# Batch 0's q as f32 at the head of SyncE's queue, ahead of two constants, in a kernel that streams weights through GpSimd's queue

## Chip, cores, metric

One core of a Trainium2 chip. The sets of rounds ran on different chips, each with its own runs of the kernel before; the traces compared below are therefore not all of one chip. The metric is device time in microseconds (us) of one execution. A profile's span is the time from its first to its last instruction, about 1.8 us less than that run's device time. KB and KB/us count 1024 bytes; the profile's GB/s count 10^9.

## The reference, cut to what matters

```python
def _attn_ref(q, k, v):                       # 8 batches, 8 heads, 576 rows, 64 wide
    phi = lambda x: np.where(x > 0, x, np.exp(x) - 1.0) + 1.0
    q_p, k_p = phi(q), phi(k)
    kv = np.einsum('bhsd,bhse->bhde', k_p, v)
    z = np.sum(k_p, axis=2)
    num = np.einsum('bhsd,bhde->bhse', q_p, kv)
    den = np.einsum('bhsd,bhd->bhs', q_p, z)[..., None] + 1e-06
    return num / den
# then, on x = the attention's rows (8, 576, 512): rfft along the rows, the first 64 modes
# each multiplied by its own complex 512 x 512 matrix (w_r, w_i), irfft, and u + relu(u @ w_ch)
```

The 128 matrices of the modes are f32 in HBM: 134 MB of the 164 MB that the profile counts as read.

## The kernel before

GpSimd's queue loads everything large, and converts from f32 to 16 bits while it loads: 24 loads for q, k and v of 8 batches, then 128 matrices. The head of the kernel:

```python
    nc.vector.memset(actwarm, 0.0)
    nc.scalar.activation(out=actwarm, in_=actwarm, func=AF.Exp)
    nc.sync.dma_start(out=id16, in_=id16_dr.ap())           # 32 KB
    nc.sync.dma_start(out=fwd_sb, in_=fwd_dr.ap())          # 160 KB
    # ... cut ...
    def load(b):
        for nm, src in (("q", q), ("k", k), ("v", v)):
            t = sA.tile([128, NHP, NJ * Dh], F16, tag=f"{nm}16", bufs=2, name=f"{nm}16_{b}")
            pin(nc.gpsimd.dma_start(out=t, in_=src[b].rearrange(...)))
            raw[nm, b] = t
    # ... cut: exps(b): ScalarE, phi = exp(raw); features(b): VectorE, raw = max(raw, 0) + 1,
    #          then phi = min(phi, raw); turn_q, sum_kv, form_x, transform: TensorE ...
    load(0)
    load(1)
    exps(0)
    for _ in features(0):
        pass
    exps(1)
    for b in range(B):
        if b + 2 < B:
            load(b + 2)
            if b >= 1:
                w_next()          # a weight matrix behind each batch's loads
        # ... cut ...
```

The modes follow: 8 + 12 buffers for the matrices, each load waiting for a buffer that TensorE has done with. In the last three modes matmuls without use fill TensorE's waits:

```python
    def keep_warm(n: int):
        for _ in range(n):
            pin(nc.tensor.matmul(last_ps[0], id16, wch16[:, 0, :]))

    FILL = {61: (2, 2, 1), 62: (5, 3, 3), 63: (6,)}
```

The last mode's product (`y_last`) is followed by the inverse transform, the relu and the stores.

## Time and profile before

| | before |
|---|---|
| time, median of 3 runs | 428.85 us (428.75 to 429.17) |
| span of the profiled run | 427.4 us |
| first byte on SyncE's queue, on GpSimd's | 1.71, 2.91 us |
| last weight byte on GpSimd's queue | 393.98 us |
| from the end of the last mode's product to the end | 32.8 us |

From the page of the kernel before, the DMA rows of its 40 slices (busy tenths, and GB/s moved), and the shares of the chain that ended last:

```profile
DMA  8999999999999999999999999999999999996698
GB/s 146 207 208 209 209 210 209 211 214 214 218 212 214 213 214 213 215 212 214 213 213 214 213 214 212 214 214 214 214 213 214 214 214 212 213 213 135 211 404 313
...
q0 software_dynamic: 32256, 82.26, 99.0%
q1 hardware_dynamic: 3568, 9.78, 6.0%
...
DMA 73%; PE 12%; DVE 6%; issue 5%; POOL 1%; ACT 1%; DVEq 0%; POOLq 0%
```

"software_dynamic" is GpSimd's queue and "hardware_dynamic" SyncE's. Only the first slice and three of the last four are not full: the first moves 146 GB/s where the later ones of the stream move 207 and more, and that is all the slack the stream has. The chain is DMA for 73%.

The timeline of the kernel before, 0 to 12 us (start, duration, engine, line, operation; in brackets the idle time before it and what ended it):

```profile
0.74 0.34 SPq L85 DMA_DIRECT2D id<-ident  x1
1.14 0.42 SPq L86 DMA_DIRECT2D fwd_sb<-dft_fwd  x1
1.26 0.90 POOL L164 DMA_DIRECT2D q<-in_q_dram  x1 [0.82 <-POOLq L820]
2.15 0.77 POOL L164 DMA_DIRECT2D k<-in_k_dram  x1
...
8.15 2.22 ACT L182 ACTIVATE qe<-q 128x1152 f16<-128x1152 f16 x2 [5.92 <-DMA q<-in_q_dram]
10.40 0.76 DVE L189 TENSOR_SCALAR q<-q 128x2304 f16<-128x2304 f16 x1 [8.89 <-ACT qe L182]
11.05 2.22 ACT L182 ACTIVATE ke<-k 128x1152 f16<-128x1152 f16 x2 [0.68 <-DMA k<-in_k_dram]
11.20 1.43 DVE L195 TENSOR_TENSOR qe<-qe,q 128x1152 f16<-128x1152 f16 x2
```

Nothing is computed before 8.15 us: q, issued first, lands only then. That is what invites the change.

The chain of the kernel before, from 388 us:

```profile
378.90 15.36 DMA wi<-in_moe_w_i_dram
394.27 0.05 issue
394.31 0.30 PE y_last L391 x4
394.61 0.02 issue
394.64 0.23 DVE YT L402
```

The last load ends at 394.27 us, and the last four matmuls of the last mode wait for it.

### The profile page before, as it was taken

To read this page: it belongs to the slowest core of one execution; us is meant where nothing else is said; L and a number is where in the kernel's file an instruction comes from. 1 tells how busy PE (TensorE), PEld (TensorE's weight loads), DVE (VectorE), ACT (ScalarE), POOL (GpSimd) and SP (SyncE) were. 2 spreads that over 40 slices of the span, in tenths; PEclk is the share of its full clock that TensorE was granted. 3 is DMA by queue.
4 is the path that set the end of the run, shared out by engine and by line. 5 is a ranking of instruction groups with operands and counts; after the bars stand their busy time and mean duration, and the time that the engine had idled before them with its cause. 6 is when DMAs were issued, how large, how long until landed. Compare 5 with 4: busy or idle time off the path is not lost.

```text
span 427.4 us, 6617 instructions
## 1 busy us (share of the span) xinstructions
PE 285.4 (67%) x2692; PEld 158.9 (37%) x2692; DVE 212.1 (50%) x432; ACT 153.7 (36%) x240; POOL 95.6 (22%) x173
## 2 busy tenths in 40 slices
PE   0357777788119765655333697777788788999991
PEld 0346655564003433333111333433333344374320
DVE  0699998956003755556200433443354344421893
ACT  3588666640102100000000244444353353431781
POOL 4233223212201322112112122122122122010600
PEclk9996666656557755555555569999898899799996
DMA  8999999999999999999999999999999999996698
GB/s 146 207 208 209 209 210 209 211 214 214 218 212 214 213 214 213 215 212 214 213 213 214 213 214 212 214 214 214 214 213 214 214 214 212 213 213 135 211 404 313
DMA packets 35854, 92.46 MB, mean 216 GB/s; under 512 B 3216, under 2 KB 16400, under 8 KB 35824
## 3 DMA queue, kind: packets, MB, share of 16 engines
q0 software_dynamic: 32256, 82.26, 99.0%
q1 hardware_dynamic: 3568, 9.78, 6.0%
q8 instruction: 21, 0.34, 0.3%
q14 instruction: 9, 0.07, 0.0%
HBM read 163.93 MB, written 9.44 MB: 406 GB/s over the span
## 4 chain that ended last, share of the span: by engine, by line
DMA 73%; PE 12%; DVE 6%; issue 5%; POOL 1%; ACT 1%; DVEq 0%; POOLq 0%
DMA wr<-in_moe_w_r_dram 48%; DMA wi<-in_moe_w_i_dram 13%; DMA pick_sb<-row_pick 4%; DMA q<-in_q_dram 4%; DMA k<-in_k_dram 4%; PE P L349 3%; PE acc L616 3%; DVE x L267 2%; PE acc L655 2%; PE z L579 1%; PE zb L606 1%; PE eps L557 1%; PE zb L605 1%; DVE qe L195 1%; ACT ke L182 1%
## 5 line engine op out<-in xcount | busy, mean ns | idle before, releaser
L349 PE MATMUL P<-wi,xt_c 128*32 128x512 bf16 x252 | 37.8, 536 | 39.7 <-DMA wi<-in_moe_w_i_dram 39.7
L360 ACT CAST ys<-P 128x512 f16<-128x512 f32 x31 | 18.2, 586 | 125.3 <-PE P L349 125.3
L110 POOL DMA_DIRECT2D wr<-in_moe_w_r_dram x64 | 34.0, 532 | 124.4 <-PE P L349 102.2
L110 POOL DMA_DIRECT2D wi<-in_moe_w_i_dram x65 | 34.5, 531 | 117.7 <-PE P L349 82.8
L358 DVE CAST ys<-P 128x512 f16<-128x512 f32 x32 | 22.1, 691 | 72.3 <-PE P L349 72.2
L349 PEld LDWEIGHTS <-xt_c 128*32 128x32 bf16 x504 | 28.9, 155 | 76.3 <-issue 65.2
L349 PE MATMUL P<-wr,xt_c 128*32 128x512 bf16 x252 | 37.5, 532 | 23.0 <-DMA wr<-in_moe_w_r_dram 20.8
L538 DVE TENSOR_TENSOR x_main<-ya,x_main 128x512 f32<-128x512 f32 x32 | 22.1, 691 | 39.7 <-PE ya L534 39.6
L557 PE MATMUL eps<-wch,xTw 128*128 128x512 f16 x144 | 41.3, 415 | 0.0
L146 PEld LDWEIGHTS <-qT 64*128 64x128 f16 (+1 forms) x640 | 23.3, 126 | 41.1 <-issue 20.7
L365 PE MATMUL yt<-pick_sb,ys 128*128 128x16 f16 x252 | 16.5, 175 | 25.5 <-DMA pick_sb<-row_pick 15.1
L540 ACT CAST x16w<-x_main 128x512 f16<-128x512 f32 x32 | 19.8, 618 | 34.7 <-DVE x_main L538 34.7
L565 ACT CAST E<-eps 128x512 f16<-128x512 f32 (+1 forms) x40 | 21.3, 543 | 26.6 <-PE eps L557 26.6
L146 PE MATMUL num<-kv,qT 64*128 64x65 f16 (+1 forms) x320 | 13.5, 223 | 22.5 <-ACT kv L242 18.7
L365 PEld LDWEIGHTS <-ys 128*128 128x128 f16 x252 | 12.2, 102 | 40.5 <-issue 17.8
L182 ACT ACTIVATE qe<-q 128x1152 f16<-128x1152 f16 x16 | 17.7, 1155 | 22.7 <-DMA q<-in_q_dram 22.7
L211 PE MATMUL qTp<-id,qe 128*128 128x128 f16 x144 | 16.8, 312 | 12.4 <-DVE qe L195 12.0
L267 DVE TENSOR_TENSOR x<-num,rd 128x512 f16<-128x512 f32 x32 | 22.1, 692 | 1.1
L146 PE MATMUL nw<-kv,qT 64*128 64x65 f16 (+1 forms) x320 | 19.6, 236 | 1.1 <-DVE x_tail L508 0.9
L211 PEld LDWEIGHTS <-qe 128*128 128x128 f16 x144 | 14.7, 147 | 13.2 <-DVE qe L195 12.0
L182 ACT ACTIVATE ke<-k 128x1152 f16<-128x1152 f16 x16 | 17.7, 1155 | 4.9 <-DMA k<-in_k_dram 4.9
L665 ACT ACTIVATE acc<-acc 128x512 f32<-128x512 f32 x34 | 18.1, 581 | 2.3 <-PE acc L616 1.7
(101 smaller groups left out, 451.8 us busy)
## 6 DMA issues: line engine op xcount, KB each, us to landing
wr<-in_moe_w_r_dram POOLq DMA_DIRECT2D x64, 512.0 KB, 18.8
wi<-in_moe_w_i_dram POOLq DMA_DIRECT2D x63, 512.0 KB, 18.9
out_dram<-x_main SPq DMA_DIRECT2D x14, 512.0 KB, 5.8
q<-in_q_dram POOLq DMA_DIRECT2D x8, 576.0 KB, 13.1
k<-in_k_dram POOLq DMA_DIRECT2D x8, 576.0 KB, 14.5
v<-in_v_dram POOLq DMA_DIRECT2D x8, 576.0 KB, 16.7
out_dram<-x_main SPq DMA_DIRECT2D x4, 256.0 KB, 3.6
out_dram<-x_tail SPq DMA_DIRECT2D x2, 512.0 KB, 5.3
```

The lines of the kernel that those rows point to most:

```text
L110: tc.keep_in_program_order(nc.gpsimd.dma_start(out=w[:, dcs], in_=rows_of[:, dcs, :]))
L146: mm = nc.tensor.matmul(num[hpo][orow, c0 : c0 + 65], qT[rows, hpp, h2, cols], kv_sb[rows, hpp, h2, :])
L182: pin(nc.scalar.activation(out=ev[:, c], in_=heads(nm, b)[:, c], func=AF.Exp))
L211: nc.tensor.transpose(qT_ps[:, j].rearrange("p t r -> p (t r)"), phi["q", b][:, hpp, j].rearrange("p o d -> p (o d)"), id16,)
L267: nc.vector.tensor_tensor(out=dst.rearrange("p (o c d) -> p o c d", o=2, c=4), in0=nv[:, :, :, 0:64], in1=rden.unsqueeze(3).broadcast_to([ ...
L349: nc.tensor.matmul(P[dc * 32 : dc * 32 + 32, :], xt_cols(dc, t, kk), w[:, dc, :], start=(t == 1), stop=(t == 0), tile_position=(0, dc * 32),)
L358: fixed(nc.vector.tensor_copy(out=st, in_=P))
L365: nc.tensor.matmul(yt_ps[:, ec, kk % 8, :], st[:, ec * 128 : ec * 128 + 128], pick_sb)
L538: pin(nc.vector.tensor_tensor(out=x, in0=acc, in1=x, op=ALU.add))
L540: pin(nc.scalar.copy(out=x16w[t], in_=x))
L557: nc.tensor.matmul(e_ps, xT[:, c, :], wch16[:, c, :], start=(c == 0), stop=(c == NDC - 1))
L565: pin(nc.scalar.copy(out=dst, in_=e_ps[:, cols]))
```

## The change

The intent: have the first q land sooner by using an empty queue, and let GpSimd begin with k. The cast to f16 is given up for this one load (in this kernel only GpSimd's loads convert), and its tiles borrow the buffers of `x16`. The diff, cut to its core:

```diff
-    nc.sync.dma_start(out=id16, in_=id16_dr.ap())
-    nc.sync.dma_start(out=fwd_sb, in_=fwd_dr.ap())
 # ...
     def load(b):
         for nm, src in (("q", q), ("k", k), ("v", v)):
+            rows_in = src[b].rearrange("h s d -> (h s) d").rearrange(
+                "(hp r j) d -> r hp (j d)", r=128, j=NJ
+            )
+            if (nm, b) == ("q", 0):
+                for c in range(2):
+                    t = sA.tile([128, 2, NJ * Dh], F32, tag="x16", bufs=2, name=f"q32_{c}")
+                    pin(nc.sync.dma_start(out=t, in_=rows_in[:, c::2, :]))
+                    raw[nm, b, c] = t
+                pin(nc.sync.dma_start(out=id16, in_=id16_dr.ap()))
+                pin(nc.sync.dma_start(out=fwd_sb, in_=fwd_dr.ap()))
+                continue
             t = sA.tile([128, NHP, NJ * Dh], F16, tag=f"{nm}16", bufs=2, name=f"{nm}16_{b}")
 # ... features(b): one max/add for each f32 half of batch 0's q instead of one for the whole tile
 # ... x16 padded from 4096 to 4608 bytes a partition, to share its buffers with q32
```

More of the change, by code (lines that the diff above doesn't have):

```diff
@@ L161, in load, with heads, flat @@
         for nm, src in (("q", q), ("k", k), ("v", v)):
-            t = sA.tile([128, NHP, NJ * Dh], F16, tag=f"{nm}16", bufs=2, name=f"{nm}16_{b}")
-            pin(
-                nc.gpsimd.dma_start(
-                    out=t,
-                    in_=src[b].rearrange("h s d -> (h s) d").rearrange(
-                        "(hp r j) d -> r hp (j d)", r=128, j=NJ
-                    ),
-                )
-            )
-            raw[nm, b] = t
-    def heads(nm, b):
-        return raw[nm, b].rearrange("p (o c) (j d) -> p c o j d", o=2, d=Dh)
+            rows_in = src[b].rearrange("h s d -> (h s) d").rearrange(
[9 more added lines that the diff above has]
+                continue
+            t = sA.tile([128, NHP, NJ * Dh], F16, tag=f"{nm}16", bufs=2, name=f"{nm}16_{b}")
+            pin(nc.gpsimd.dma_start(out=t, in_=rows_in))
+            raw[nm, b] = t
+    def heads(nm, b, c):
+        if (nm, b) == ("q", 0):
+            return raw[nm, b, c].rearrange("p o (j d) -> p o j d", d=Dh)
+        return raw[nm, b].rearrange("p (o c) (j d) -> p c o j d", o=2, d=Dh)[:, c]
+    def flat(nm, b):
+        tiles = [raw[nm, b, c] for c in range(2)] if (nm, b) == ("q", 0) else [raw[nm, b]]
+        return [t.rearrange("p a f -> p (a f)") for t in tiles]
     def exps(b):
@@ L181, in exps @@
             for c in range(2):
-                pin(nc.scalar.activation(out=ev[:, c], in_=heads(nm, b)[:, c], func=AF.Exp))
+                pin(nc.scalar.activation(out=ev[:, c], in_=heads(nm, b, c), func=AF.Exp))
     def features(b):
         for nm in ("q", "k"):
-            rf = raw[nm, b].rearrange("p a f -> p (a f)")
             ev = phi[nm, b].rearrange("p c j o d -> p c o j d")
-            pin(
-                nc.vector.tensor_scalar(
-                    out=rf, in0=rf, scalar1=0.0, scalar2=1.0, op0=ALU.max, op1=ALU.add
+            for rf in flat(nm, b):
+                pin(
+                    nc.vector.tensor_scalar(
+                        out=rf, in0=rf, scalar1=0.0, scalar2=1.0, op0=ALU.max, op1=ALU.add
+                    )
                 )
-            )
             for c in range(2):
@@ L195, in features @@
                     nc.vector.tensor_tensor(
-                        out=ev[:, c], in0=ev[:, c], in1=heads(nm, b)[:, c], op=ALU.min
+                        out=ev[:, c], in0=ev[:, c], in1=heads(nm, b, c), op=ALU.min
                     )
@@ L252, in form_x @@
             x16s[b] = (
-                sA.tile([128, NJJ, D], F16, tag="x16", bufs=2, name=f"x16_{b}"),
+                sA.tile([128, 2 * NJ * Dh * 2], F16, tag="x16", bufs=2, name=f"x16_{b}")[
+                    :, 0 : NJJ * D
+                ].rearrange("p (j d) -> p j d", j=NJJ),
                 sA.tile([128, D], F16, tag="x16t", bufs=2, name=f"x16t_{b}"),
```

## The prediction

> **What bounds the kernel.** The time before is 428.85 us (span 427.4 us). The chain that ended last is 73% DMA, nearly all of it loads of the mode weights. In the trace's DMA records GpSimd's queue moves its first byte at 2.91 us and its last weight byte at 393.98 us, and between these one of its packets is always under way: 391 us of gapless stream. After it come 33 us of TensorE and stores. So only two things can move the end: when the stream starts, and how much work the 16 DMA engines do in it. Attention is not on this path: VectorE is full from 30 to 95 us, but modes 0 and 1 are multiplied at 105 us, and mode 0's rows then wait for a 4 KB constant that queues behind the weights until 127 us (timeline, chain).
>
> **What the change does to the stream.** It takes batch 0's q out: 512 packets. In the steady part 512 packets of q, k or v take 2.84 us. The first 512 took 4.07 us: the stream starts slowly, 43, 104, 153 KB/us in the three half microseconds from 3.0, against 203 later; about 1.2 us are lost.
> It puts the same elements on SyncE's queue as f32. They are read as f32 either way; the casting stream writes 203 KB/us (406 read), and the f32 stores of the last stage run at 396 KB/us, so I estimate 1152 KB at about 395 KB/us: 2.9 us. The work isn't less, it is moved. The Trainium skill says so too ("DMA: Bandwidth & Descriptors", Issuing engines are not separate DMA queues): all queues run on the same 16 engines and interleave. The trace before doesn't show it.
> The gain is what falls into idle time. SyncE's bytes flow from 1.71 us, 1.2 us before GpSimd's; the constants (192 KB, about 0.6 us at full rate) are hidden there now. They come behind q and then compete. Estimate: 3.5 us of work, of which 0.9 us fits before 2.91 us and 0.6 to 1.2 us into the slow start; the rest delays GpSimd's stream by 1.4 to 2.0 us, against 2.84 us taken out. Net 0.8 to 1.4 us.
>
> **What it adds off the path.** VectorE: q's max/add becomes two f32 halves, its min two f32 operations. The skill ("VectorE: DVE Perf Modes", Mode 2×_2P) has f32 tensor_tensor at one element per cycle, so I estimate 1.25 us instead of 0.72 for each min, and 0.65 to 0.7 us for each half of the max (now 0.76 for both): 1.7 us in all, where VectorE idles for 8.9 us. The exponentials stay 1.11 us. GpSimd issues one load less (0.9 us), but still starts at 1.26 us. q of batch 2 no longer waits for a buffer (until 12.0 us); the stream was full anyway. Instruction order is otherwise unchanged on all engines.
>
> **Prediction.** 427.8 us, 8 times in 10 between 427.0 and 428.8. Faster by over 2%: 1%; within 2%: 98%; slower: 1%.
>
> **Signs.** First exponential of q at 4.5 to 5.5 us (now 8.15), of k at 8 to 9.5 (now 11.05); attention ends some 2 us earlier (now 104), worth nothing; GpSimd's first byte still near 2.9 us, its last near 392.9; tail still 33 us.
>
> **What would make it wrong.** SyncE's q flowing slower than 395 KB/us or starting late (no gain, or a loss of tenths); arbitration that starves GpSimd's start; a gap opening in the stream; a tail whose clock is granted differently.

## The result

| | before | changed |
|---|---|---|
| time, median of 4 runs, same rounds | 429.01 us (428.75 to 429.75) | 429.07 us (428.74 to 429.7) |
| ratio (95% interval) | | 1.000 (0.9982 to 1.0018) |
| span of the profiled run | 427.4 us | 427.1 us |
| GpSimd's first byte | 2.91 us | 5.33 us |
| GpSimd's last weight byte | 393.98 us | 392.64 us |
| modes 0 and 1 multiplied from | 104.86 us | 102.77 us |

A ratio is the mean time of one kernel's runs over that of the other's in the same rounds, so it is not quite the ratio of the medians quoted beside it.

No change is to be seen in these four runs, and 429.07 lies outside the predicted range. The same rows of the changed kernel's page:

```profile
DMA  9999999999999999999999999999999999996697
GB/s 216 207 208 209 209 210 209 212 212 216 217 213 214 212 214 214 213 213 214 213 214 213 214 213 215 213 214 213 216 213 213 213 215 213 212 214 127 219 408 303
...
q0 software_dynamic: 31728, 81.67, 98.1%
q1 hardware_dynamic: 4112, 10.96, 6.8%
...
DMA 66%; PE 16%; DVE 7%; issue 6%; ACT 1%; POOL 1%; DVEq 0%; POOLq 0%; ACTq 0%
```

The first slice is now full (216 GB/s, but f32 counts twice as many written bytes as f16 for the same elements, so this row alone doesn't say how much of the stream was saved). The same stretch of the timeline:

```profile
0.74 0.95 SPq L166 DMA_DIRECT2D q<-in_q_dram  x2
...
1.26 0.90 POOL L172 DMA_DIRECT2D k<-in_k_dram  x1 [0.81 <-POOLq L830]
1.74 0.46 SPq L168 DMA_DIRECT2D id<-ident  x1
...
4.71 1.16 ACT L190 ACTIVATE qe<-q 128x1152 f16<-128x1152 f32 x1 [2.48 <-DMA q<-in_q_dram]
5.91 0.76 DVE L197 TENSOR_SCALAR q<-q 128x1152 f32<-128x1152 f32 x1 [4.39 <-ACT qe L190]
...
8.05 2.62 DVE L203 TENSOR_TENSOR qe<-qe,q 128x1152 f16<-128x1152 f16 x2
...
9.67 2.21 ACT L190 ACTIVATE ke<-k 128x1152 f16<-128x1152 f16 x2 [2.32 <-DMA k<-in_k_dram]
```

The intent is met: q's first exponential starts at 4.71 us instead of 8.15, k's at 9.67 instead of 11.05. Each f32 min takes 1.31 us against 0.72 for f16, which agrees with the Trainium skill ("VectorE: DVE Perf Modes", Mode 2×_2P: f32 tensor_tensor stays at one element per cycle).

And the end of the chain, from 388 us:

```profile
391.75 0.47 PE y_last L401 x16
392.22 1.30 PE zl L345 x6
393.52 0.49 PE y_last L401 x16
394.00 0.02 issue
394.03 0.24 DVE YT L412
```

In this execution the last mode no longer waits for its load. TensorE comes to it at 393.35 us, behind its filling matmuls (`zl`), 0.2 us before the last bytes land (393.55). In the repeat a1_same it waits again. Over all 16 traces the last product ends 0.33 to 0.68 us after the last landing, 0.33 where its last four matmuls wait for it; in the three of the changed kernel 0.33 to 0.44, so TensorE holds the end up by 0.1 us there at most.

The start of both streams, in two stretches (length; busy us and count of PE, PEld, DVE, ACT, POOL; granted clock, DMA share, GB/s), the kernel before and then the changed one:

```profile
1.00:3.00 2.00, 0.00 (x0) 0.00 (x0) 0.52 (x2) 1.22 (x2) 1.74 (x3) 1.00 0.40 98
3.00:6.00 3.00, 0.00 (x0) 0.00 (x0) 0.00 (x0) 0.00 (x0) 2.89 (x4) 1.00 1.04 141
```

```profile
1.00:3.00 2.00, 0.00 (x0) 0.00 (x0) 0.52 (x2) 1.22 (x2) 1.74 (x3) 1.00 0.49 82
3.00:6.00 3.00, 0.00 (x0) 0.00 (x0) 0.09 (x1) 1.16 (x1) 2.89 (x4) 1.00 1.06 371
```

SyncE's q moves less in the head than the small constants did: 82 GB/s against 98. In the packet records 124 KB of its 1152 had been started by 2.91 us (112 and 166 KB in the two repeats of the changed kernel below). Only after 3 us does it flow at full rate, and until 5.33 us GpSimd's queue moves nothing.

### A better ruler than the time

Differences of some tenths drown in runs that differ by 1 us. The records of each load's completion tell more. A load is announced by 16 increments of a semaphore, one for each DMA engine; the Trainium skill says why ("DMA: Bandwidth & Descriptors", Why a DMA increments its semaphore by 16 and not by 1): the engines finish independently, and only the full 16 mean that the data is there. From here on, "landing" is the pair of first and last increment of the very last weight load, the 128 KB piece. The first increment is the steadier one: it belongs to the engine that is furthest ahead, and the change moved it by 0.51 to 0.60 us in three executions. Two kernels told below that differ from these only at the other end, b_halffill and a_halffill, have it 0.16 us earlier and 0.09 to 0.18 us later, so a difference under some 0.2 us says nothing. The last belongs to the slowest engine, which trails by 3.5 to 4.8 us there and jumps by over half a microsecond from one execution to another. The last mode waits for the last increment; the ruler used here for what the change does to the stream is the first. It is not the only one possible: the mean of the 16 increments moved by 0.64, 0.73 and 0.87 us in the three executions. The increments and packets are read from the trace's records; no view of the profile prints them.

All kernels at a glance. The landings and spans are those of the one profiled execution of each; times and ratios are from all its runs.

```
kernel        GpSimd's    landing, us        span   median   ratio to before
              first byte  first    last      us     us       (95% interval)
before        2.91        389.99   394.27    427.4  -        1
changed       5.33        389.39   393.55    427.1  429.07   1.0000 (0.9982 to 1.0018)
a1_same       5.25        389.48   392.94    426.5  428.74   0.9985 (0.9967 to 1.0004)
a2_same       5.23        389.40   392.88    426.6  428.79   0.9989 (0.9975 to 1.0002)
b_q0free      2.94        387.00   390.56    424.3  426.35   0.9926 (0.9909 to 0.9942)
b_halffill    2.92        389.83   394.07    428.9  430.52   1.0018 (1.0001 to 1.0035)
a_halffill    5.47        389.57   393.10    428.7  430.29   1.0020 (1.0005 to 1.0034)
a_late        2.99        390.84   394.66    428.9  430.32   1.0035 (1.0012 to 1.0059)
a_constfirst  3.85        389.76   393.58    427.6  429.39   1.0002 (0.9989 to 1.0015)
a_half        3.86        389.31   393.94    427.2  428.46   0.9980 (0.9966 to 0.9993)
a_half2       4.01        389.30   392.80    425.9  427.97   0.9964 (0.9940 to 0.9988)
a_half_act    4.26        389.03   392.64    426.1  428.08   0.9969 (0.9945 to 0.9994)
a_q32gp       2.87        390.75   394.32    428.3  430.02   1.0010 (0.9986 to 1.0033)
b_constlate   2.87        390.56   394.81    428.0  429.73   1.0005 (0.9977 to 1.0033)
b_q16x2       2.83        390.09   394.90    428.7  430.15   1.0019 (1.0006 to 1.0032)
a_full_act    5.64        389.30   393.24    426.8  428.73   0.9993 (0.9979 to 1.0006)
```

### The profile page after: what moved, and what is told of

Same layout as the page of the kernel before. It is cut to its first block, busy times and chain, and to the rows that moved or that the text cites. A ratio compares the mean times of both kernels' runs of the same rounds, so it can differ in the third digit from the quotient of the medians.

```text
span 427.1 us, 6622 instructions
## 1 busy us (share of the span) xinstructions
PE 281.3 (66%) x2692; PEld 159.1 (37%) x2692; DVE 214.3 (50%) x433; ACT 154.0 (36%) x240; POOL 94.5 (22%) x172
## 4 chain that ended last, share of the span: by engine, by line
DMA 66%; PE 16%; DVE 7%; issue 6%; ACT 1%; POOL 1%; DVEq 0%; POOLq 0%; ACTq 0%
DMA wi<-in_moe_w_i_dram 48%; DMA wr<-in_moe_w_r_dram 9%; DMA k<-in_k_dram 9%; PE P L359 3%; PE acc L626 3%; PE acc L665 2%; DVE x L277 2%; PE z L589 2%; PE zl L345 1%; ACT ke L190 1%; PE yp L602 1%; PE zb L616 1%; DVE ke L203 1%; PE zb L615 1%; DVE k L197 1%
## 5 line engine op out<-in xcount | busy, mean ns | idle before, releaser
L359 PE MATMUL P<-wi,xt_c 128*32 128x512 bf16 x252 | 36.5, 521 | 43.3 <-DMA wi<-in_moe_w_i_dram 43.3
L359 PE MATMUL P<-wr,xt_c 128*32 128x512 bf16 x252 | 36.6, 521 | 25.0 <-DMA wr<-in_moe_w_r_dram 22.9
L567 PE MATMUL eps<-wch,xTw 128*128 128x512 f16 x144 | 39.6, 401 | 0.0
L190 ACT ACTIVATE qe<-q 128x1152 f16<-128x1152 f16 (+1 forms) x16 | 17.8, 1156 | 17.7 <-DMA q<-in_q_dram 17.7
```

What stands on the lines that cost most here:

```text
L190: pin(nc.scalar.activation(out=ev[:, c], in_=heads(nm, b, c), func=AF.Exp))
L359: nc.tensor.matmul(P[dc * 32 : dc * 32 + 32, :], xt_cols(dc, t, kk), w[:, dc, :], start=(t == 1), stop=(t == 0), tile_position=(0, dc * 32),)
L567: nc.tensor.matmul(e_ps, xT[:, c, :], wch16[:, c, :], start=(c == 0), stop=(c == NDC - 1))
```

## The experiments

The theory after the first result: the stream did move, by 0.6 us, and that reaches the end, but four runs cannot show it; it is less than predicted because of a term at the head of the stream. Rivals: the move is lost to TensorE or the tail; or the prediction's 1 us is there and the runs were unlucky.

### The change again: a1_same, a2_same

No edit.

> The changed kernel again, to size its effect. Theory S (the stream moved by 0.6 us, and this reaches the end): faster than before by 0.3 to 0.7 us, ratio 0.9985 to 0.9993; GpSimd's first byte again near 5.3 us; the first engine to finish the last weight load does so near 389.4 us (before 389.99). Rival N (nothing reaches the end; TensorE's own work or the tail hides it): ratio within 0.9996 to 1.0004 at the same landing. Rival P (the prediction's size was right and the four runs were unlucky): ratio 0.9970 to 0.9981.

> The changed kernel a third time, beside the other orders of the head on one chip, so that the differences between them have their own baseline, and to narrow the interval of its effect. Theory S: 0.3 to 0.7 us faster than before, ratio 0.9985 to 0.9993. Rival N: 0.9996 to 1.0004.

Measured: 428.74 against 429.36 us, ratio 0.9985, and 428.79 against 429.18 us, ratio 0.9989. Both lie at the edge between the theory and "nothing" as far as the intervals go, each of which just includes 1. Over all 15 runs of the changed kernel the mean is 428.88 us, over the 26 of before in the same three sets of rounds 429.32: 0.44 us less, give or take 0.35 (two standard errors). The prediction's 1 us is excluded by neither interval alone, but the first increment moved by 0.51 and 0.59 us, not by 0.8 to 1.4 (the mean increment by 0.73 and 0.87). So there is an effect, of about half a microsecond, somewhat more by the mean increment. That the first four runs were a poor draw fits this; nothing else shows it.

### Does a shorter stream reach the end? b_q0free

Batch 0's q is not loaded, its tile is set to zero. Its output is wrong, which doesn't matter for the time.

```diff
+            if (nm, b) == ("q", 0):
+                pin(nc.vector.memset(t, 0.0))
+                raw[nm, b] = t
+                continue
             pin(
                 nc.gpsimd.dma_start(
```

> The kernel before with batch 0's q not loaded at all, its tile set to zero on VectorE; wrong result on purpose. It takes 512 packets out of GpSimd's queue and adds none anywhere. Theory S (one for one): the first engine's landing of the last load 2.8 us earlier (387.2 against 389.99), time 2.4 to 3.0 us down, ratio 0.9930 to 0.9944. Rival N (TensorE's backlog in modes 57 to 62 or the tail decides): landing 2.8 us earlier, time down by 0.6 us or less, ratio 0.9986 or more.

Measured: 426.35 against 429.36 us, ratio 0.9926; landing 387.00 us, 2.99 earlier. The chain of this kernel, from 385 us:

```profile
376.12 14.45 DMA wi<-in_moe_w_i_dram
390.56 0.05 issue
390.61 0.30 PE y_last L395 x4
```

The load is last here too, as in the kernel before. One for one, as the theory has it, by the first increment. (In the two profiled executions the last increment moved by 3.71 us and the span by 3.2, so there the tail took 0.5 us longer; why is open.) The rival that TensorE or the tail swallows the gain falls, and the step of the prediction that the stream decides the time stands. The experiment also sets the zero of the scale: a cast q costs the stream 2.99 us, and the change's q with its later constants 2.39 to 2.48 us (389.39 to 389.48 less 387.00).

It shows where these 2.4 us lie, too. From GpSimd's first byte to the first increment of the last load the stream takes 384.05 us in b_q0free and 384.06, 384.23 and 384.17 us in the changed kernel and its repeats (by the mean increment 385.84, and 385.91, 385.90 and 385.78). So the whole cost of the moved q and its later constants is the later start of GpSimd's queue, 5.23 to 5.33 us instead of 2.94; from there on it costs the stream nothing that can be seen.

### Do the filling matmuls hold the end? b_halffill, a_halffill

The chain of the changed kernel ended in filling matmuls. Both kernels with 9 of them in place of 22:

```diff
-    FILL = {61: (2, 2, 1), 62: (5, 3, 3), 63: (6,)}
+    FILL = {61: (1, 1, 0), 62: (2, 1, 1), 63: (3,)}
```

> The kernel before with 9 instead of 22 filling matmuls in the last three modes, 2.8 us less on TensorE ahead of the last mode's product. Theory S: the last mode waits for its last load either way (landing 394.27 us), so no change beyond 0.2 us, ratio 0.9995 to 1.0005, unless the waits cost TensorE its clock. Rival N (TensorE sets the end): 0.4 us or more faster, ratio 0.9990 or less.

> The changed kernel with the same 9 filling matmuls. In the changed kernel's trace the last product began 0.2 us ahead of the last landing, so TensorE and the loads were level. Theory S: the same as the changed kernel within 0.3 us (ratio to before 0.9982 to 0.9993). Rival N (fillers hide the gain): 0.6 us or more faster than the changed kernel of the same rounds, and the first chip run of the change would be explained by TensorE.

Measured: both about 0.2% slower than before (ratios 1.0018 and 1.0020), and 1.5 us slower than the change with all its fillers (430.29 against 428.74 us, medians of the same rounds). The stretches of the kernel before and then of b_halffill, from 388 to 400 us (length, then busy us and count of PE, PEld, DVE, ACT, POOL; then the granted clock, DMA share and GB/s):

```profile
388.00:394.00 6.00, 5.95 (x58) 2.56 (x57) 1.32 (x2) 0.00 (x0) 0.00 (x0) 1.00 0.64 123
394.00:400.00 6.00, 5.29 (x41) 2.98 (x38) 2.88 (x6) 3.27 (x7) 2.77 (x6) 1.00 0.19 63
```

```profile
388.00:394.00 6.00, 3.59 (x41) 1.55 (x40) 1.32 (x2) 0.00 (x0) 0.00 (x0) 0.80 0.61 116
394.00:400.00 6.00, 5.47 (x27) 2.89 (x28) 2.31 (x5) 2.28 (x5) 1.93 (x4) 0.63 0.05 16
```

With less filling TensorE is busy for 3.59 us of the six before 394 instead of 5.95, and is granted 0.63 instead of 1.00 of its clock in the six after. The clock record has one half-speed stretch there, 391.6 to 398.5 us, where the kernel before has none between 375.7 and 420.0. The first matmuls of the tail show it (kernel before, then b_halffill):

```profile
395.15 1.04 PE L757 MATMUL zl<-wch,YT 128*128 128x256 f16 x8
```

```profile
395.12 1.91 PE L757 MATMUL zl<-wch,YT 128*128 128x256 f16 x8
```

So the "unless" of the expectation came true. The Trainium skill describes this clock ("TensorE: Matmul & The Clock Gate", What's actually happening: half rate after an idle window of about 3.4 us, full rate after a busy one), and the trace agrees with the length: its stretches last 3.41 us or multiples of it. It does not take a wholly idle window: in the 3.4 us before the half-speed stretch of b_halffill TensorE was busy for 1.27 us, and its longest wait near there was 1.47 us. For the question at hand this experiment is spoiled by the clock: a_halffill's last product waited for its load (begun 392.51 us, last landing 393.10), but the slower tail outweighs whatever that won. What settles it is the 0.1 us found above, the most that TensorE holds the end up in the changed kernel with all its fillers. So they don't hide the gain, and they earn their place.

### What does q as f32 cost where nothing is idle? a_late

The constants first, and q's two loads behind a write of their tiles on VectorE:

```diff
+                pin(nc.sync.dma_start(out=id16, in_=id16_dr.ap()))
+                pin(nc.sync.dma_start(out=fwd_sb, in_=fwd_dr.ap()))
                 for c in range(2):
                     t = sA.tile([128, 2, NJ * Dh], F32, tag="x16", bufs=2, name=f"q32_{c}")
+                    pin(nc.vector.memset(t, 0.0))
                     pin(nc.sync.dma_start(out=t, in_=rows_in[:, c::2, :]))
                     raw[nm, b, c] = t
-                pin(nc.sync.dma_start(out=id16, in_=id16_dr.ap()))
-                pin(nc.sync.dma_start(out=fwd_sb, in_=fwd_dr.ap()))
```

> The changed kernel, but SyncE takes the two constants first and q's two loads wait for VectorE to write the same tiles, to about 3.5 us. So no byte of q falls into the idle head. Theory W (only idle time is won): GpSimd's first byte back near 2.9 us; q's 2.9 us of f32 work now competes with the stream; the first engine's landing of the last load within 0.3 us of before (389.99), time as before, ratio 0.9994 to 1.0008. Rival Q (the gain comes from fewer packets in GpSimd's queue, not from the head): landing as in the changed kernel, 389.4 or less, ratio 0.999 or less. In the overlap, both queues move bytes in every half microsecond if the engines share; one of them stands still if not.

Measured: slower than before, ratio 1.0035 (433.45 us, one of its six runs, weighs on this; without it the means differ by 1.0 us instead of 1.6); landing 390.84 us. Neither number was expected: theory W is right that the gain is gone, but the stream lost 390.84 - 387.00 = 3.84 us, not 2.9 to 3.0.

Not all of it is the price of the f32 load. Later in the trace GpSimd issues a load late (its line of the timeline), and the stream dips (two stretches, as above; the last figure is GB/s):

```profile
21.67 1.11 POOL L173 DMA_DIRECT2D k<-in_k_dram  x1 [15.78 <-DVE ke L204]
```

```profile
20.00:24.00 4.00, 2.34 (x38) 2.04 (x37) 3.97 (x7) 3.77 (x4) 1.85 (x2) 1.00 1.21 208
24.00:25.00 1.00, 0.21 (x1) 0.11 (x1) 0.96 (x2) 0.98 (x3) 0.53 (x1) 1.00 1.08 131
```

With q late, VectorE frees k's buffer late, so GpSimd issues its seventh load at 21.67 us (12.63 in b_q0free, 14.67 in the changed kernel). The sixth lands at 24.38 us, and the dip from 208 to 131 GB/s follows. The increments of the loads around it put this dip at 0.49 us. That leaves 3.35 us for an f32 q beside the stream: 0.4 more than the cast q.

While both queues run (7 to 12 us in the records) GpSimd's moves 92 to 104 KB/us and SyncE's 166 to 202: they share, but twice GpSimd's plus SyncE's is about 381 KB/us of f32 read, against 406 when GpSimd's runs alone. In the changed kernel little of q ran beside the stream: its last packet ended at 5.76 us, 0.43 after GpSimd's first byte.

A second surprise: SyncE issued the first of these loads at 2.75 us, and its first byte moved at 6.65.

### The type, the number of loads, the queue: a_q32gp, b_q16x2

a_q32gp is the change with q's two f32 loads on GpSimd's queue and the constants back at the head of SyncE's:

```diff
-                    pin(nc.sync.dma_start(out=t, in_=rows_in[:, c::2, :]))
+                    pin(nc.gpsimd.dma_start(out=t, in_=rows_in[:, c::2, :]))
```

> Only the type of the change: batch 0's q as two f32 loads, but on GpSimd's queue, the constants at the head of SyncE's queue as before. Nothing falls into the idle head. With q absent the first engine's landing of the last load was 387.00 us, with q cast to f16 389.99. Theory W: 512 packets of f32 cost what the cast ones do (2.8 to 3.1 us), landing 389.7 to 390.4, time within 0.4 us of before. Rival F (f32 in itself is dearer, as the 3.8 us of the late q suggest): landing 390.6 to 391.0 and 0.6 us or more slower than before.

Measured: landing 390.75 us; 430.02 against 429.18 us. By the landing this is rival F: on the very same queue the f32 q costs 3.75 us and the cast q 2.99. The first 512 packets of k behind it took 4.25 us, where 512 take 2.84 in the steady part, so the slow start of the casting stream was paid behind the f32 load as well. The increments show that this is all of the 0.76 us: the two f32 loads landed at 6.71 us (first increment), no later than the cast q of the kernel before (6.80), and k 3.69 us after them, where it takes 2.85 in the kernel before. So the f32 load itself was not dearer here; the casting load behind it was.

b_q16x2 is the kernel before with batch 0's q in two loads, still cast:

```diff
+                for c in range(2):
+                    pin(nc.gpsimd.dma_start(out=t[:, c::2, :], in_=rows_in[:, c::2, :]))
```

> The kernel before with batch 0's q as two loads of half the size on GpSimd's queue, still cast to f16. If the extra 0.76 us of the f32 loads on this queue come from the type: landing of the last load as before, 389.9 to 390.1, no change of time beyond 0.2 us. If they come from two loads in place of one: landing 390.5 to 390.8 and 0.5 us or more slower.

Measured: landing 390.09 us, 0.10 later than before. So it is the change of type in the queue and not the number of loads. The time was not as expected: 430.15 against 429.15 us, ratio 1.0019. In its profile the slowest engine trails the first by 4.81 us (before 4.28), and its last increment, 394.90 us, is the latest of all kernels. That fits the longer time, but why this engine fell back is open.

### What do the constants cost? b_constlate, a_constfirst, a_full_act

b_constlate is the kernel before with the constants behind some writes on VectorE:

```diff
+    tc.keep_in_program_order(nc.vector.memset(wch16, 0.0))
+    tc.keep_in_program_order(nc.vector.memset(wch16, 0.0))
+    tc.keep_in_program_order(nc.vector.memset(id16, 0.0))
+    tc.keep_in_program_order(nc.vector.memset(fwd_sb, 0.0))
     nc.sync.dma_start(out=id16, in_=id16_dr.ap())
```

> The kernel before with only the two constants moved out of the idle head: SyncE waits for VectorE, to about 3.2 us, so that they flow at about 4 us beside GpSimd's stream. It prices the term 'constants compete', which the prediction put at 0.6 us. Theory W: landing of the last load 390.3 to 390.7 against 389.99, time 0.3 to 0.8 us up. If small packets hide between the large ones: landing within 0.1 us of 390.0, no change.

Measured: landing 390.56 us, so they cost 0.57 us beside the stream; the prediction's 0.6 was right. Time 429.73 against 429.18 us; the interval includes 1. Again the first byte was late: issued at 3.68 us, moved at 7.84.

a_constfirst is the change with the two constants ahead of q instead of behind it (the two lines moved up).

> The changed kernel with the two constants ahead of q in SyncE's queue, as they were before the change. The same bytes on each queue in another order. Theory W: same work in the same head, so the landing of the last load 389.2 to 389.7 and the time within 0.3 us of the changed kernel; GpSimd's first byte at 5.3 to 6.0 us, as all of SyncE's bytes come first. Rival C (small constant packets beside GpSimd's stream cost more than in the head): 0.3 to 0.6 us faster than the changed kernel, landing near 389.0.

Measured: landing 389.76 us, 0.28 to 0.37 later than the change, and no gain in time (1.0002). Both expectations missed: the order matters, and the other way round than rival C had it. q's first byte came at 2.83 instead of 1.84 us, so q ran beside the stream (to 9.88 us), where it costs more (a_late). GpSimd's first byte came at 3.85 us, not at 5.3 to 6.0.

a_full_act is the change with the constants at the head of ScalarE's queue:

```diff
+    nc.scalar.dma_start(out=id16, in_=id16_dr.ap())
+    nc.scalar.dma_start(out=fwd_sb, in_=fwd_dr.ap())
     nc.vector.memset(actwarm, 0.0)
```

> The changed kernel with only the two constants moved to the head of ScalarE's queue. With half of q the same move brought the landing from 389.31 to 389.03. If the constants are a term of their own: landing 389.0 to 389.2 (changed kernel 389.39 to 389.48), 0.2 to 0.5 us faster than the changed kernel's ratio of 0.9985 to 0.9989. If not: 389.4 and the same time as the changed kernel. Either way the half version stays the better one (389.03), as f32 is dearer than the cast.

Measured: landing 389.30 us, 0.09 to 0.18 earlier than the change, ratio 0.9993. A miss: the difference is within what the ruler varies by, and the time shows nothing.

### Half of it: a_half, a_half2, a_half_act

Half of batch 0's q on SyncE as f32, the other half first on GpSimd as f16:

```diff
-                for c in range(2):
-                    t = sA.tile([128, 2, NJ * Dh], F32, tag="x16", bufs=2, name=f"q32_{c}")
-                    pin(nc.sync.dma_start(out=t, in_=rows_in[:, c::2, :]))
-                    raw[nm, b, c] = t
+                t = sA.tile([128, 2, NJ * Dh], F32, tag="x16", bufs=2, name="q32_0")
+                pin(nc.sync.dma_start(out=t, in_=rows_in[:, 0::2, :]))
+                raw[nm, b, 0] = t
+                t = sA.tile([128, NHP, NJ * Dh], F16, tag="q16", bufs=2, name="q16_0")[:, 0:2, :]
+                pin(nc.gpsimd.dma_start(out=t, in_=rows_in[:, 1::2, :]))
+                raw[nm, b, 1] = t
```

> Half of batch 0's q (two of its four row groups) on SyncE as f32, the other half first in GpSimd's queue as f16. SyncE's data is half as long (590 KB, 1.5 us at 392 KB/us). If GpSimd's first packet waits until what SyncE has queued before it is through: first byte at 3.8 to 4.3 us (changed kernel 5.3, before 2.9). If its lateness has a fixed cause: 5.3 again. Stream: theory W says that the idle head is already filled by this half, so the landing of the last load is 389.2 to 389.7, as in the changed kernel; if the gain goes with the packets taken out, only half of 0.6 us.

> The half version again, on one chip with its variant, to see whether its 0.7 us against before (ratio 0.998) stand. If it is the best version: ratio 0.9970 to 0.9988. If it was luck: like the changed kernel, 0.9985 to 0.9993.

a_half_act also has the constants at the head of ScalarE's queue, as in a_full_act:

> Half of q as f32 on SyncE's queue and half as f16 on GpSimd's, and the two constants at the head of ScalarE's queue, so that they and q both start at about 1.7 us. Theory W (the head has room for only some 0.5 us of work, whatever the queue): landing 389.1 to 389.5, the same as with the constants behind q (389.31). If two queues fill the slow start better than one: 388.9 or less, and 0.3 us or more faster than the half alone.

Measured: GpSimd's first byte at 3.86 and 4.01 us with half the f32 data, 5.2 to 5.6 with all of it, 2.8 to 3.0 with none ahead: its lateness grows with what SyncE has queued before it, so it is no fixed delay. That is not the whole rule: in a_constfirst all of q was queued as well, behind the constants, and GpSimd's first byte came at 3.85 us. What decides there is open. The f32 data itself was through at 4.16 and 4.15 us (with the whole q in the changed kernel at 5.5 to 5.8). Landing 389.31 and 389.30: the half saves the stream no less than the whole. The times are 428.46 against 429.18 us (0.9980) and 427.97 against 429.18 (0.9964); both intervals exclude 1. (The 432.55 us run of before is in the second set, and in that of a_q32gp, b_constlate and a_half_act; without it a_half2's ratio of means is 0.9972.) With the constants on ScalarE's queue the landing is 389.03, 0.28 earlier and between its two expectations, and the time 428.08 against 429.18 us (0.9969), in those rounds no better than the half alone. These are the fastest versions that give the right result, by 0.7 to 1.2 us over the kernel before. That is under 2%.

## Why the prediction was wrong, point by point

It said 427.8 us, a gain of 1.05 us. Measured were +0.06 us in the first four runs, and -0.62 and -0.39 in the next sets of rounds.

- **What bounds the kernel: right.** b_q0free took 2.99 us off the stream and 3.0 us off the time. In every kernel with all its fillers the span ends 33.1 to 34.2 us after the last landing.
- **q's cost as a cast load, 2.84 us: right** (2.99). **The constants' 0.6 us: right** (0.57 in b_constlate).
- **"I estimate 1152 KB at about 395 KB/us: 2.9 us": right for q as it ran here**, alone on the engines: 394 to 402 KB/us from 3 to 5 us in the three executions. Beside the stream it would have been 3.35 us (a_late).
- **"0.9 us fits before 2.91 us": this is the step that failed.** SyncE's bytes did flow from 1.84 us, but slowly: 112 to 166 KB of q were started by 2.91 us, worth 0.3 to 0.4 us at 395 KB/us. The prediction took nearly the full rate from the start; 0.9 us of it would be 355 KB. The kernel before could have warned: its SyncE queue had 175 KB of constants under way by then, and the profile shows 98 GB/s. Why the queue begins slowly is open.
- **"0.6 to 1.2 us into the slow start": about the lower end.** GpSimd's first casting load took 3.89 us from first byte to first increment in both kernels (2.85 in the steady part), in the changed one with all 192 KB of constants beside it. So the constants fitted into the slow start, and of q only what flowed in its last 0.43 us.
- **"The rest delays GpSimd's stream by 1.4 to 2.0 us": it was 2.4 to 2.5 us**, as follows from the two terms: of 3.5 us of work some 0.3 and 0.6 us fitted, not 1.5 to 2.1, which leaves an estimated 2.6. Against the 2.99 us taken out, the 2.4 to 2.5 us leave the 0.51 to 0.60 us that the first increment shows. This is a sum over the record; no run changes the slow beginning of SyncE's queue alone.
- **"GpSimd's first byte still near 2.9 us": wrong**, 5.3 us. The prediction took the two queues to interleave from the first moment. The Trainium skill says they take turns packet by packet ("DMA: Bandwidth & Descriptors", Queues, rings and completion order). The traces agree once both are running (a_late), but not at the start: the first bytes of whichever queue comes second came late, as if behind much of what the other had outstanding (a_constfirst does not fit), 2.4 us for GpSimd in the changed kernel, and about 4 us from issue for SyncE in a_late and b_constlate. The engines are busy meanwhile (371 GB/s from 3 to 6 us in the changed kernel), so the wait itself idles little; it is q's remaining work that costs.
- **Signs off the path:** right for q's first exponential (4.71 us), for attention's end some 2 us earlier and worth nothing, for the tail (33.1 us). k's exponential came a little late (9.67 us, predicted 8 to 9.5). VectorE's extra work was 1.95 us, predicted 1.7: each f32 half of the max took 0.76 us, not 0.65 to 0.7.
- **The range was also too narrow for the noise.** Before's own median was 428.85 us when the prediction was made, and 429.01 to 429.36 in the later sets; single runs spread over 1 us and more. In the first profile the slowest engine trailed by 4.16 us, in the two repeats by 3.46 and 3.48, and the spans follow: 427.1, 426.5, 426.6 us. What makes an engine fall back in one execution and not in another was not settled.

## What to carry to other kernels

When a kernel is bound by one gapless stream of transfers, a load moved to another queue wins only what that queue moves while the stream would have idled. Measure how much it moves there, byte by byte, instead of taking its later rate from the start; here it was a third to a half of the estimate. Price the load by taking it away altogether in one experiment. Put no more into an idle head than fits it; here half of the load on the second queue did as much for the stream as all of it, and the time fell. When an experiment prices something by the end of a long stream, look for other dips on the way: one of 0.49 us sat in a_late. And when the effect is smaller than the spread of the runs, look for an event in the trace that moves with the cause and not with the noise: here the first engine's completion of the last load was good to about 0.2 us, where the time was good to 0.5.

## What the Trainium skill lacked or had wrong

- "DMA: Bandwidth & Descriptors", Queues, rings and completion order: it has the engines take turns between queues packet by packet. It lacks how long a queue that joins late waits for its first packet: GpSimd's first byte came at 5.3 us instead of 2.9 behind 1152 KB on SyncE's queue and at 3.9 to 4.0 behind half of that; SyncE's came 3.9 us (a_late) and 4.2 us (b_constlate) after issue behind GpSimd's stream. The amount queued ahead is not all of it: 3.85 us in a_constfirst.
- The same page, Issuing engines are not separate DMA queues: it says that the queues share the engines, which the runs confirm, but not that sharing costs throughput: about 381 KB/us of f32 read in a_late while a plain and a casting load ran together, against 406 for the casting stream alone.
- The same page, Specifications: it gives a first-byte latency of about 1 us for GpSimd's path and 0.6 us for SyncE's. It does not say from where it counts. From the start of the issuing instruction the first byte took 1.65 us (1.26 to 2.91) and 0.97 us (0.74 to 1.71) in the kernel before, from its end 0.75 and 0.63 us.
- No page that we read says how slowly a queue's bytes begin to flow after the first one: 112 to 166 KB of f32 on SyncE's queue in the 1.1 us to 2.91 us, where 394 to 402 KB/us followed. Nor has one the price of such a load beside a casting stream: 3.35 us of the stream for 1152 KB (a_late, its dip taken off), where the same elements cast to f16 cost 2.99.
- The same page, Why a DMA increments its semaphore by 16 and not by 1: it says that the engines finish independently, but not how far they drift apart in a long stream: 1.3 us at the first load and 4.3 us at the last in the kernel before.
- "TensorE: Matmul & The Clock Gate", What's actually happening: it lacks how little work counts as an idle window. b_halffill's half-speed stretch (391.6 to 398.5 us, two windows of 3.41 us) followed one in which TensorE was busy for 1.27 us of 3.4, with no wait over 1.47 us near it.
